# The last item of an attention taken in two parts, with the second part's row maxima beside the first part's exponentials

## The chip, the cores and the metric

The kernel runs on one core of one Trainium2 chip. The metric is device time in microseconds (us) of one execution, as the median over several. TensorE (PE in the profile) multiplies matrices into PSUM, of which there are eight banks of 128 x 512 fp32; VectorE (DVE), ScalarE (ACT) and GpSimd (POOL) work element by element; SyncE (SP) issues the DMA transfers here. Each engine works off its own instructions in order and waits for the others by semaphores.

## The reference

One transformer layer on 2048 rows of 512 columns: 32 heads of 16 columns, and an MLP of 1792 columns with SiLU.

```python
h  = x + softmax_attention(layernorm(x) @ wqkv) @ wo    # 32 heads of 16, scale 1/4
h2 = h + silu(layernorm(h) @ w1) @ w2
```

The softmax is over all 2048 keys, so every query row of every head needs the maximum of 2048 scores before its exponentials.

## The kernel before, in words

Everything is one program of three stages that overlap: layer norm and the projections to q, k and v; the attention; and, for each block of 512 rows (NB = 4), the output projection with wo and the MLP. The attention of the next block runs on around the output of the block before, in one order written out by hand in Python (`for g in range(groups)`, L1049 on).

**Items, groups, chunks.** The attention is cut into 32 *items* (ITEMS): four heads by one block of 512 query rows. An item is 16 *groups*, one for each *chunk* c of 128 keys (KC = 16); group g is chunk g % 16 of item g // 16. A group makes, for its four heads k (HEADS gives each head's place a, j in the tiles), a score product (`scores`, L395: 128 keys x 512 queries into a PSUM bank ps_s, 64 rows of the array) and an exponential on ScalarE into a tile pt; and, two groups later (LAG), four value products (`values`, L656) that add pt into the bank pv, one head in each 32 of its partitions. Row DH of each head's 32 is the sum of the exponentials. After chunk 15 `finish_item` (L671) copies pv to pvs.

**Maxima.** Before an item's exponentials its 64 *maxima* have to be there: `maximum` (L222) multiplies 128 queries by 512 keys of one head in natural order into ps_m (48 rows of the array) and VectorE reduces the 512 columns to one (into mx). j says which half of the array's rows a head uses; a score product and a maximum with the other j can run in the array at the same time. When an item's 64 are found, `finish_max` (L235) takes the maximum over the four key blocks, either on GpSimd, or, where it is urgent, on VectorE (L241), and splits it in two fp16 parts; `place_max` (L264) transposes these, copies them into mt and writes them by two DMAs (L276) into rows 48 and 49 of q's tile qs, so that the score product subtracts them. `due_at` (L306) sets when: jointly in a coming chunk 2 (JOINT), or, if there is none in time, WAIT = 2 steps after the last maximum was found.

**Where maxima stand.** A planner, `maxima(g)` (L1029), says how many (up to three, two in chunk 2) are put beside the four scores of group g: it takes the largest rate at which some coming item would be ready in time, counting off what is set beside the outputs (BESIDE). With three, they stand behind scores 0 to 2, or, if the half (j) that comes first has fewer left than the other, behind scores 1 to 3 (`skip`, L1092). Beside an output's MLP (`mlp`, L823) they stand in bursts: per part f of FC = 14, three after the fifth and three after the last of twelve products (BESIDE_C), and four in the second product, one of those in the bank pv; only in parts f < QUIET of that block, which is 14, 14 and 13. The MLP stands ahead of chunk 0 of items 9, 17 and 25 (`marks`: groups 144, 272, 400), its output projection beside the groups just before.

**The end.** The last item (31) has no maxima beside it. Its VectorE splits the attention's rows of the last block into two fp32r parts (`split_early`) in chunks 0 to 3 and the first two weights w1 in chunk 9. Behind its last group, `finish_last` (L905) transposes pvs, divides by the sums, transposes back (ps_q, o_t, ps_o), makes the last rows of hth and htl of it, projects with wo (ps_wo), and runs the last block's MLP with nothing beside it.

PSUM banks: four for ps_s (`st`), three for ps_m and ps_n (`sm`), one for pv.

Of the kernel before, what the change touches and what calls it, by code (L numbers as in the profile page):

```python
# [48 lines left out]
ITEMS = NB * H // 4  # L49

FIRSTS = 8, 16, 24

# [5 lines left out]

BESIDE = (135, 135, 124)
OUTPUT = 9  # L60
# [12 lines left out]

QUIET = FC, FC, FC - 1


@with_exitstack
def attention_mlp_kernel(ctx: ExitStack, tc: tile.TileContext, x, wqkv, wo, w1, w2, out):
# [134 lines left out]
    def fixed_rows(i):  # L213
        for j in range(2):
# [3 lines left out]
                fix_k[:, None, :].to_broadcast([16, 8, 512]))  # L218

    mx, left = {}, {}  # L220

    def maximum(i, kb, qt, a, j, ps=None):  # L222

        if i not in mx:
            mx[i] = small.tile([P, 2, 2, 4, 4], F32, name="mx", bufs=RING + 1)
            left[i] = 64
# [4 lines left out]
        pin(nc.vector.tensor_reduce(mx[i][:, j, a, qt, kb:kb + 1], ps, axis=AX.X, op=ALU.max))  # L231
        left[i] -= 1
        return left[i] == 0

    def finish_max(i, urgent):  # L235

        nm = small.tile([P, 16], F32, name="nm")
        m4 = mx.pop(i).rearrange("p j a q k -> p (j a q) k")
# [11 lines left out]
        ns = small.tile([P, 2, 2, 8], F16, name="ns")  # L250
        high, rest = (ns[:, :, r, :] for r in range(2))
# [4 lines left out]
        split[i] = ns  # L256

# [5 lines left out]

    def place_max(i):  # L264

        ns = split.pop(i)
        ps = bank("ps_n", "sm", F16)
        tr(ps[:32, :P], ns.rearrange("p j r a -> p (j r a)"), ident_h)
        mt = small.tile([32, P], F16, name="mt")
        if at["attention"]:  # L270
            dve("tensor_copy", mt, ps[:32, :P])
        else:
            act("copy", mt, ps[:32, :P])
# [3 lines left out]
        placed.add(i)  # L277

# [26 lines left out]

    def due_at(i):  # L306
# [5 lines left out]
        return joint - g if joint < KC * i - 2 and joint // KC - 1 not in (-1, *FIRSTS) else WAIT  # L312

    def one_max(half=None, ps=None):

        i = next_item()
        if i == ITEMS:
            return
        if half is None:
            half = at["half"]  # L320
            at["half"] = 1 - half
        if at["blocks"]:

            i = min(range(2), key=lambda n: (todo[n, half] or todo[n, 1 - half] or [(n, KC)])[0][1])
# [5 lines left out]
        found_all = maximum(*todo[i, half].pop(0), ps)  # L330

        finish_rest()
        if found_all:
            steps = due_at(i)
            g = at["group"]
            if g is None or g + 1 in marks:
                soon(steps, place_max, i)
                finish_max(i, g is not None)
                return
            late.setdefault(at["step"] + steps, []).append(i)  # L340
            if steps == WAIT:
                unfinished.append(i)
                found_at["step"] = at["step"]
            else:
                finish_max(i, False)

# [21 lines left out]
    def scores(g, k, kind="st"):  # L368

        i, c = divmod(g, KC)  # L370
        a, j = HEADS[k]
        assert i in placed
# [283 lines left out]
    def values(g):  # L656
        i, c = divmod(g, KC)
        for k in range(4):
            a, j = HEADS[k]
            mm(pv[32 * k:32 * k + DH + 1, :], va[:, c, 4 * (i % 8) + 2 * a + j, :], pts.pop((g, k)),  # L660
               start=c == 0, stop=c == KC - 1)
        if c == KC - 1:
            finish_item(i)

    def place(i, k):
# [5 lines left out]
    def finish_item(i):  # L671

        b, u = divmod(i, 8)
        pvs = bp.tile([P, 512], F32, name="pvs", bufs=1)
        if i == ITEMS - 1:
# [6 lines left out]
        if i == ITEMS - 1:  # L682
            last.append(pvs)
            return
# [10 lines left out]

    rcs, last = {}, []

    def sums(i):
# [206 lines left out]
    def finish_last(pending):  # L905
        b = NB - 1
        for g in pending:
            values(g)
        pvs = last.pop()

        o_t = pt_tile("o_t").rearrange("p (t n) -> p t n", n=P)
        pool("memset", o_t[:, :, :64], 0.0)
        act("activation", small.tile([P, 1], F32, name="sw"), ident[:, :1], AF.Silu)
# [10 lines left out]
        some(0, 3)  # L924
        ps_q, ps_o = (bank(name).rearrange("p (t n) -> p t n", n=P) for name in ("ps_q", "ps_o"))
        for t in range(4):
            tr(ps_q[:, t, :], pvs[:, t * P:(t + 1) * P], ident)
        rc = small.tile([P, 4, 4], F32, name="rl", bufs=1)
        heads = ps_q.rearrange("p t (k r) -> p t k r", r=32)
        dve("reciprocal", rc, heads[:, :, :, DH])  # L930
        for j in range(2):

            to = o_t[:, :, 64:].rearrange("p t (k d) -> p t k d", d=DH)[:, :, 1 - j::2, :]
            dve("tensor_tensor", to, heads[:, :, j::2, :DH],
                rc[:, :, j::2, None].to_broadcast([P, 4, 2, DH]), ALU.mult)
        some(0, 6)
        for t in range(4):
            tr(ps_o[:, t, :], o_t[:, t, :], ident)
        ps_o = ps_o.rearrange("p t n -> p (t n)")[64:]
        act("copy", hth[64:, DC - 1, :], ps_o)  # L940
        low(htl[64:, DC - 1, :], ps_o, hth[64:, DC - 1, :])
        found, parts = {}, {}
# [86 lines left out]
    def maxima(g):  # L1029

        i, c = divmod(g, KC)
        ready = min(ITEMS, i + RING - (0 if c == KC - 1 else 1)) * 64
        rate = max([(64 * (n + 1) - sum(x for x, m in zip(BESIDE, marks) if g <= m <= KC * n) - at["done"])
                    / max(1, KC * n - AHEAD - g) for n in range(i + 1, ITEMS)] or [0])
        if ready < END:
# [13 lines left out]
    for g in range(groups):  # L1049
# [11 lines left out]
        if i in FIRSTS:  # L1061
# [11 lines left out]
            if c == 13:  # L1073
                split_weights("w1", 0, "pool")
        if i == ITEMS - 1:
            if c < 4:
                load_rows(NB - 1, c)
                split_early(c)
            if c == 4:
                for f in range(3):  # L1080
                    load_weights("w1", f)
                load_weights("w2", 0)
                for f in range(2):
                    soon(5, split_weights, "w1", f, "dve", "dve")
        if g == 1:
# [3 lines left out]

        half = 1 - HEADS[g % 2][1]  # L1090
        j = next_item()
        skip = int(n == 3 and j < ITEMS and len(todo[j, half]) < len(todo[j, 1 - half]))  # L1092
        for m in range(4):
            k = m ^ (g % 2)
            if (g, k) not in pts:
                scores(g, k)
            if skip <= m < skip + n:
                one_max(1 - HEADS[k][1])
        if found_at["step"] < at["step"]:
# [45 lines left out]
```

## Time and profile before

| what | us |
|---|---|
| median of 3 runs (1670.39 to 1671.31) | 1670.42 |
| the profiled execution | 1670.46 |
| its span, first to last instruction | 1668.4 |
| PE busy in the span | 1655.0 |
| VectorE busy | 1448.6 |
| ScalarE busy | 1236.4 |
| preparation, up to the first group's scores | 180.5 |
| third output with its MLP, 1215.0 to 1347.7 | 132.7 |
| items 25 to 30, 1347.7 to 1538.4 | 190.7 |
| item 31, 1538.4 to 1571.0 | 32.6 |
| last output and MLP, 1571.0 to 1668.4 | 97.4 |

Times in the views count from the span's start. In a row of the time-ordered view stand the start, the time until the last of the merged instructions ends, the engine, the line, the operation, out<-in, and how many; L85 is the helper that issues every matrix product, L88 every transpose, L102 VectorE's and L99 ScalarE's operations, so that rows are told apart by their tiles. The durations of PE's instructions overlap, since they are pipelined; the distance between starts is what one takes. A row of the windows has the stretch, its length, the busy time of PE, PE's weight loads, VectorE, ScalarE and GpSimd with the number of instructions, the granted clock, and the DMA engines' share and GB/s.

### The profile page before, as it was taken

The numbers are of one execution on the slowest core, as the hardware profiler recorded it, in microseconds if no ns is written. First come the engines' busy times: TensorE is split into PE (matmuls) and PEld (weight loads), VectorE is DVE, ScalarE is ACT, GpSimd is POOL, SyncE is SP. The second block draws the span as 40 slices with busy tenths as digits, with TensorE's granted clock in tenths as the row PEclk, the third lists the DMA queues.
The fourth block names the chain that finished last, engine by engine and source line by source line (L and its number), as shares of the span: only waits on it lengthen the run. The fifth ranks groups of instructions, "written<-read, shape, count | busy, mean of one in ns | idle before, by whom it ended". The sixth has DMA issues, their size and how long they took to land.

```text
span 1668.4 us, 28544 instructions
## 1 busy us (share of the span) xinstructions
PE 1655.0 (99%) x10542; PEld 648.1 (39%) x10542; DVE 1448.6 (87%) x2391; ACT 1236.4 (74%) x2435; POOL 399.0 (24%) x593
## 2 busy tenths in 40 slices
PE   9999999999999999999999999999999999999999
PEld 7666422222245532222245532222245532222387
DVE  7899999999988889999988889999978889997343
ACT  5323799999952389999952279999963279999743
POOL 5423311211234301211244301211234311211200
PEclk9999999999999999999999999999999999999999
DMA  5434411211232211111232111121232111100222
GB/s 199 107 99 140 120 32 37 58 32 37 66 78 67 58 50 35 42 49 33 62 79 74 58 50 32 38 56 32 61 75 80 58 50 32 35 12 21 65 77 81
DMA packets 104403, 102.83 MB, mean 62 GB/s; under 512 B 22732, under 2 KB 81164, under 8 KB 104264
## 3 DMA queue, kind: packets, MB, share of 16 engines
q1 hardware_dynamic: 104264, 101.02, 22.3%
q8 instruction: 82, 1.34, 0.3%
q14 instruction: 57, 0.47, 0.1%
HBM read 77.72 MB, written 17.29 MB: 57 GB/s over the span
## 4 chain that ended last, share of the span: by engine, by line
PE 89%; ACT 5%; DVE 4%; issue 1%; DMA 1%; POOL 0%; SPq 0%; DVEq 0%; POOLq 0%
PE pv L85 34%; PE ps_s L85 20%; PE ps_m L85 11%; PE ps_acc L85 10%; PE ps_qk L85 5%; ACT pt L99 5%; PE ps_wo L85 3%; PE ps_w L85 3%; PE ps_v L85 3%; DVE mx L231 2%; PE ps_tr L88 1%; DVE pvs L102 0%; PE ps_n L88 0%; DVE st L102 0%; SPq L105 0%
## 5 line engine op out<-in xcount | busy, mean ns | idle before, releaser
L231 DVE TENSOR_REDUCE mx<-ps_m 128x1 f32<-128x512 f32 x2009 | 1258.8, 684 | 83.3 <-PE ps_m L85 55.7
L99 ACT ACTIVATE pt<-ps_s 128x512 f32<-128x512 f32 x2048 | 1011.6, 609 | 31.6 <-PE ps_m L85 18.7
L85 PE MATMUL pv<-pt,va 128*17 128x512 f32 x4096 | 537.5, 598 | 1.7 <-DVE pv L102 0.5
L85 PE MATMUL ps_s<-qs,ks 64*128 64x512 f16 x2048 | 531.1, 379 | 3.0 <-ACT pt L99 1.6
L85 PE MATMUL ps_m<-ks,qs 48*128 48x512 f16 x2009 | 501.7, 380 | 0.8 <-DVE mx L231 0.7
L85 PEld LDWEIGHTS <-ks 64*128 64x128 f16 x2048 | 148.6, 95 | 546.9 <-issue 437.6
L92 POOL TENSOR_TENSOR ri<-rc,minus 128x16 f32<-128x16 f32 x31 | 90.6, 2923 | 344.6 <-DMA rc<-dn 344.6
L85 PEld LDWEIGHTS pv<-pt,va 128*17 128x17 f32 x4096 | 68.8, 95 | 217.9 <-issue 204.4
L85 PEld LDWEIGHTS <-qs 48*128 48x128 f16 x2048 | 117.5, 94 | 66.6 <-issue 62.2
L99 ACT CAST w2h<-w 128x512 fp32r<-128x512 f32 x56 | 34.7, 620 | 102.3 <-PE ps_acc L85 102.3
L99 ACT ACTIVATE g<-pv 128x512 f32<-128x512 f32 x39 | 23.3, 597 | 101.9 <-PE pv L85 101.9
L85 PE MATMUL ps_acc<-w2l,gh 128*128 128x512 f32 x224 | 92.9, 415 | 0.0
L85 PE MATMUL ps_acc<-w2h,gh 128*128 128x512 f32 x224 | 92.4, 413 | 0.0
L92 POOL TENSOR_TENSOR w2l<-w,w2h 128x512 fp32r<-128x512 f32 x42 | 53.8, 1282 | 152.7 <-ACT w2h L99 152.7
L85 PE MATMUL ps_acc<-w2h,gl 128*128 128x512 f32 x224 | 88.1, 393 | 0.0
L102 DVE TENSOR_TENSOR gl<-g,gh 128x512 fp32r<-128x512 f32 x53 | 37.1, 700 | 46.7 <-ACT gh L99 46.7
L99 ACT ACTIVATE ks<-ps_qk,qk_s 128x512 f32<-128x512 f32 x30 | 20.7, 690 | 68.8 <-PE ps_qk L85 66.8
L85 PE MATMUL pv<-htl,w1h 128*128 128x512 f32 x156 | 65.6, 420 | 0.0
L85 PE MATMUL pv<-hth,w1h 128*128 128x512 f32 x156 | 62.5, 401 | 0.0
L85 PE MATMUL pv<-hth,w1l 128*128 128x512 f32 x156 | 61.4, 393 | 0.0
L92 POOL TENSOR_SCALAR nm<-nm 128x16 f32<-128x16 f32 x51 | 13.0, 254 | 191.5 <-DVE nm L241 188.2
L92 POOL TENSOR_TENSOR mx<-mx 128x32 f32<-128x32 f32 x38 | 9.5, 250 | 199.1 <-DVE mx L231 197.5
(135 smaller groups left out, 1439.2 us busy)
## 6 DMA issues: line engine op xcount, KB each, us to landing
w<-in_B_w_dram SPq DMA_DIRECT2D x112, 256.0 KB
ks<-kd SPq DMA_DIRECT2D x120, 192.0 KB
qs<-qd SPq DMA_DIRECT2D x128, 48.0 KB
kd<-sh SPq DMA_DIRECT2D x16, 256.0 KB
qd<-sh SPq DMA_DIRECT2D x16, 256.0 KB
hx<-in_A_x_dram SPq DMA_DIRECT2D x16, 256.0 KB
ot<-pvs SPq DMA_DIRECT2D x124, 32.0 KB
den<-dr SPq DMA_DIRECT2D x124, 32.0 KB
```

The source lines that it names most:

```text
L85: tc.keep_in_program_order(nc.tensor.matmul(*a, **k))
L88: tc.keep_in_program_order(nc.tensor.transpose(*a))
L92: tc.keep_in_program_order(getattr(nc.gpsimd, op)(*a, **k))
L99: pin(getattr(nc.scalar, fn)(*a, **k))
L102: pin(getattr(nc.vector, fn)(*a, **k))
L231: pin(nc.vector.tensor_reduce(mx[i][:, j, a, qt, kb:kb + 1], ps, axis=AX.X, op=ALU.max))
```

## The change

Three things, all of them in the order of work; what is computed stays.

1. Item 31 (LAST) is taken in two parts of eight groups: heads with a = 0, then heads with a = 1. A group of it has two heads and two chunks of keys instead of four heads and one chunk (`head`), so that pv holds each head twice, for even and odd chunks. Each part has its own 32 maxima (a *piece*), its own hand-over (nm and ns of 8 and 16 columns, a DMA that writes only that part's half of qs), and its own due time. The first part's pv is copied (`finish_part`), transposed, added, divided and turned back inside the second part (`divide_part`, `turn_part`); `finish_last` does the same for the second part, where it had one division for four heads.
2. The planner's goals: item 31's first 32 maxima are due at its chunk 0, the others at its chunk 8. BESIDE for the third output is 103 in place of 124, and its QUIET 11 in place of 13.
3. With two maxima in a group, and more left in the half that is first, both go to that half, behind scores 0 and 2. The shift with three stays as it was.

In item 31 `split_early` moves from chunks 0 to 3 to chunks 5 to 8, and the two splits of w1 from chunk 9 to chunks 12 and 13.

```diff
-BESIDE = (135, 135, 124)
+BESIDE = (135, 135, 103)
-QUIET = FC, FC, FC - 1
+QUIET = FC, FC, FC - 3
...
+    def head(g, k):
+        i, c = divmod(g, KC)
+        if i < LAST:
+            return *HEADS[k], c
+        return c // HALF, k % 2, c % HALF * 2 + k // 2
+
+    def piece_of(i, a):
+        return i, a if i == LAST else None
...
         for j in range(2):
-            dst = qs[i % RING][64 * j + 48:64 * j + 50].rearrange("r a n -> r (a n)")
-            pin(nc.sync.dma_start(dst.rearrange("r (a b) -> r a b", b=P), mt[16 * j:16 * j + 16, :]))
+            dst = qs[i % RING][64 * j + 48:64 * j + 50, slice(None) if a is None else slice(a, a + 1)]
+            dst = dst.rearrange("r a n -> r (a n)").rearrange("r (a b) -> r a b", b=P)
+            pin(nc.sync.dma_start(dst, mt[n // 2 * j:n // 2 * (j + 1), :]))
...
+    def finish_part():
+        pvs = bp.tile([P, 512], F32, name="pvs", bufs=1)
+        dve("tensor_copy", pvs, pv)
+        o_t = gp.tile([P, 4, P], F32, name="o_t", tag="oh")
+        pool("memset", o_t, 0.0)
+        last.append(o_t)
+        soon(2, divide_part, 0, pvs, o_t, "sm")
+        soon(4, turn_part, 0, o_t, "sm", "dve")
+
+    def divide_part(part, pvs, o_t, kind="st"):
+        ps = bank("ps_q", kind).rearrange("p (t n) -> p t n", n=P)
+        for t in range(4):
+            tr(ps[:, t, :], pvs[:, t * P:(t + 1) * P], ident)
+        halves = ps.rearrange("p t (m j r) -> p t m j r", m=2, r=32)[:, :, :, :, :DH + 1]
+        both = gp.tile([P, 4, P], F32, name="both", tag="ol")[:, :, :2 * (DH + 1)].rearrange("p t (j r) -> p t j r", j=2)
+        rc = small.tile([P, 4, 2], F32, name="rl", bufs=1)
+        dve("tensor_copy", both, halves[:, :, 0])
+        dve("tensor_tensor", both, halves[:, :, 1], both, ALU.add)
+        dve("reciprocal", rc, both[:, :, :, DH])
+        to = o_t[:, :, 64 + 32 * part:96 + 32 * part].rearrange("p t (j d) -> p t j d", j=2)
+        dve("tensor_tensor", to, both[:, :, :, :DH], rc[:, :, :, None].to_broadcast([P, 4, 2, DH]), ALU.mult)
+
+    def turn_part(part, o_t, kind="st", engine="act"):
+        ps = bank("ps_o", kind)
+        for t in range(4):
+            tr(ps[:, t * P:(t + 1) * P], o_t[:, t, :], ident)
+        rows = slice(64 + 32 * part, 96 + 32 * part)
+        if engine == "act":
+            act("copy", hth[rows, DC - 1, :], ps[rows])
+        else:
+            dve("tensor_copy", hth[rows, DC - 1, :], ps[rows])
+        low(htl[rows, DC - 1, :], ps[rows], hth[rows, DC - 1, :])
...
-        ps_q, ps_o = (bank(name).rearrange("p (t n) -> p t n", n=P) for name in ("ps_q", "ps_o"))
...
+        divide_part(1, pvs, o_t)
         some(0, 6)
...
+        turn_part(1, o_t)
...
+        goals = [(64 * (n + 1), KC * n) for n in range(i + 1, LAST)]
+        goals += [(END - 32 * (1 - a), KC * LAST + HALF * a) for a in range(2) if KC * LAST + HALF * a > g]
...
-        skip = int(n == 3 and j < ITEMS and len(todo[j, half]) < len(todo[j, 1 - half]))
+        more = len(todo[j, half]) - len(todo[j, 1 - half]) if j < ITEMS else 0
+        beside = range(n)
+        if n == 3 and more < 0:
+            beside = range(1, 4)
+        if n == 2 and more > 0:
+            beside = 0, 2
```

More of the change, by code (lines that the diff above doesn't have):

```diff
@@ L49 @@
 ITEMS = NB * H // 4
+LAST = ITEMS - 1
+HALF = KC // 2
 FIRSTS = 8, 16, 24
@@ L218, in fixed_rows, with start_of @@
                 fix_k[:, None, :].to_broadcast([16, 8, 512]))
+    def head(g, k):
[5 more added lines that the diff above has]
+        return i, a if i == LAST else None
+    def start_of(piece):
+        i, a = piece
+        return KC * i + HALF * (a or 0)
     mx, left = {}, {}
     def maximum(i, kb, qt, a, j, ps=None):
-        if i not in mx:
-            mx[i] = small.tile([P, 2, 2, 4, 4], F32, name="mx", bufs=RING + 1)
-            left[i] = 64
+        piece = piece_of(i, a)
+        n = 1 if i == LAST else 2
+        if piece not in mx:
+            mx[piece] = small.tile([P, 64], F32, name="mx", bufs=RING + 1)[:, :32 * n].rearrange(
+                "p (j a q k) -> p j a q k", j=2, a=n, k=4)
+            left[piece] = 32 * n
         if ps is None:
@@ L230, in maximum, with finish_max @@
            ks[i % RING][64 * j:64 * j + 48, a, kb * 512:kb * 512 + 512], start=True, stop=True)
[L231 to L238, printed above, removed]
+        pin(nc.vector.tensor_reduce(mx[piece][:, j, a % n, qt, kb:kb + 1], ps, axis=AX.X, op=ALU.max))
+        left[piece] -= 1
+        return left[piece] == 0
+    def finish_max(piece, urgent):
+        m4 = mx.pop(piece).rearrange("p j a q k -> p (j a q) k")
+        rows = m4.shape[1]
+        nm = small.tile([P, 16], F32, name="nm")[:, :rows]
         sign = 1.0
@@ L249, in finish_max @@
                 pool("tensor_tensor", to, to, a, ALU.add)
-        ns = small.tile([P, 2, 2, 8], F16, name="ns")
-        high, rest = (ns[:, :, r, :] for r in range(2))
+        ns = small.tile([P, 32], F16, name="ns")[:, :2 * rows]
+        high, rest = (ns.rearrange("p (j r a) -> p j r a", j=2, r=2)[:, :, r, :] for r in range(2))
         nm = nm.rearrange("p (j a) -> p j a", j=2)
@@ L255, in finish_max @@
         pool("tensor_tensor", rest, nm, high, ALU.subtract)
-        split[i] = ns
+        split[piece] = ns
     placed, split, unfinished, found_at = set(), {}, [], {"step": 0}
@@ L304, in next_item, with due_at @@
         return at["item"]
-    def due_at(i):
+    def due_at(piece):
         g = at["group"]
@@ L311, in due_at @@
         joint = g + WAIT + (JOINT - g - WAIT) % KC
-        return joint - g if joint < KC * i - 2 and joint // KC - 1 not in (-1, *FIRSTS) else WAIT
+        return joint - g if joint < start_of(piece) - 2 and joint // KC - 1 not in (-1, *FIRSTS) else WAIT
     def one_max(half=None, ps=None):
@@ L329, in one_max @@
         at["done"] += 1
-        found_all = maximum(*todo[i, half].pop(0), ps)
+        block = todo[i, half].pop(0)
+        piece = piece_of(i, block[3])
+        found_all = maximum(*block, ps)
         finish_rest()
         if found_all:
-            steps = due_at(i)
+            steps = due_at(piece)
             g = at["group"]
             if g is None or g + 1 in marks:
-                soon(steps, place_max, i)
-                finish_max(i, g is not None)
+                soon(steps, place_max, piece)
+                finish_max(piece, g is not None)
                 return
-            late.setdefault(at["step"] + steps, []).append(i)
+            late.setdefault(at["step"] + steps, []).append(piece)
             if steps == WAIT:
-                unfinished.append(i)
+                unfinished.append(piece)
                 found_at["step"] = at["step"]
             else:
-                finish_max(i, False)
+                finish_max(piece, False)
     def burst(n, *more):
@@ L368, in scores @@
     def scores(g, k, kind="st"):
-        i, c = divmod(g, KC)
-        a, j = HEADS[k]
-        assert i in placed
+        i = g // KC
+        a, j, c = head(g, k)
+        assert piece_of(i, a) in placed
         ps = bank("ps_s", kind)
@@ L908, in finish_last @@
             values(g)
-        pvs = last.pop()
-        o_t = pt_tile("o_t").rearrange("p (t n) -> p t n", n=P)
-        pool("memset", o_t[:, :, :64], 0.0)
+        o_t, pvs = last
         act("activation", small.tile([P, 1], F32, name="sw"), ident[:, :1], AF.Silu)
@@ L924, in finish_last @@
         some(0, 3)
-        ps_q, ps_o = (bank(name).rearrange("p (t n) -> p t n", n=P) for name in ("ps_q", "ps_o"))
[L926 to L935, printed above, removed]
-        some(0, 6)
[L937 to L941, printed above, removed]
+        divide_part(1, pvs, o_t)
+        some(0, 6)
+        turn_part(1, o_t)
         found, parts = {}, {}
@@ L1096, in attention_mlp_kernel @@
                 scores(g, k)
-            if skip <= m < skip + n:
-                one_max(1 - HEADS[k][1])
+            if m in beside:
+                one_max(1 - head(g, k)[1])
         if found_at["step"] < at["step"]:
```

42 lines of the change are left out of this document (24 added, 18 removed).

## The prediction

> **What bounds the kernel now.** I read the page first, then the time-ordered view of TensorE (PE) in one part of an MLP and in the attention, the last item of the attention over all engines, the windows by stage, and the chain of waits behind the last item.
>
> ```profile
> span 1668.4 us, 28544 instructions
> PE 1655.0 (99%) x10542; PEld 648.1 (39%) x10542; DVE 1448.6 (87%) x2391; ACT 1236.4 (74%) x2435; POOL 399.0 (24%) x593
> ```
>
> PE is never idle for long, so what counts is how much PE time each piece takes and what it sits beside. A maximum (a score product into ps_m, then a VectorE reduce into mx) has two very different prices, depending on where it stands.
>
> Beside an output's MLP, where every other product uses the whole array, a burst of maxima is inserted time:
>
> ```profile
> 1329.74 0.39 PE L85 MATMUL pv<-htl,w1h 128*128 128x512 f32 x1
> 1330.06 0.60 PE L85 MATMUL ps_m<-ks,qs 48*128 48x512 f16 x3
> 1330.93 0.40 PE L85 MATMUL ps_acc<-w2h,gl 128*128 128x512 f32 x1
> ...
> 1332.34 0.40 PE L85 MATMUL ps_acc<-w2h,gl 128*128 128x512 f32 x1
> 1332.67 0.60 PE L85 MATMUL ps_m<-ks,qs 48*128 48x512 f16 x3
> 1333.54 0.40 PE L85 MATMUL ps_acc<-w2h,gh 128*128 128x512 f32 x1
> ...
> 1342.01 0.40 PE L85 MATMUL pv<-hth,w1h 128*128 128x512 f32 x1
> 1344.81 0.40 PE L85 MATMUL ps_acc<-w2h,gh 128*128 128x512 f32 x1
> ```
>
> The last two rows stand twelve products apart with nothing between: (1344.81 - 1342.01)/12 = 0.233 us each. From 1329.74 to 1330.93 there are two such steps and a burst of three: 1.19 - 0.47 = 0.72 us. From 1332.34 to 1333.54 two steps and a burst of four (the fourth goes into the bank pv): 1.20 - 0.47 = 0.73 us. So a burst costs 0.73 us, whether of three or four.
>
> In the attention a maximum is free on PE: it runs in the half of the array's rows that the score product beside it leaves empty. There the clock is the group of four scores, three maxima and four value products:
>
> ```profile
> 1417.67 0.39 PE L85 MATMUL ps_s<-qs,ks 64*128 64x512 f16 x2
> 1419.63 0.39 PE L85 MATMUL ps_s<-qs,ks 64*128 64x512 f16 x1
> 1419.86 0.59 PE L85 MATMUL ps_s<-qs,ks 64*128 64x512 f16 x2
> 1420.25 0.37 PE L85 MATMUL ps_m<-ks,qs 48*128 48x512 f16 x1
> 1421.76 0.39 PE L85 MATMUL ps_s<-qs,ks 64*128 64x512 f16 x1
> ...
> 224.22 0.39 PE L85 MATMUL ps_s<-qs,ks 64*128 64x512 f16 x1
> 226.35 0.39 PE L85 MATMUL ps_s<-qs,ks 64*128 64x512 f16 x1
> ...
> 1388.21 0.39 PE L85 MATMUL ps_s<-qs,ks 64*128 64x512 f16 x1
> 1390.17 0.39 PE L85 MATMUL ps_s<-qs,ks 64*128 64x512 f16 x1
> ```
>
> A group takes 1.96 us (1388.21 to 1390.17, chunk 4 of item 26; 1417.67 to 1419.63, chunk 3 of item 27). But chunk 4 of item 27 takes 2.13 us (1419.63 to 1421.76): its third maximum starts at 1420.25, 0.62 after the group's first score, where two slots of 0.23 (1419.63 to 1419.86) would put it at 0.46. That group follows one in which the maxima were shifted by one place (two scores first, in the row 1417.67), so six maxima come with one pause too few, VectorE falls behind, and the third waits for one of the three ps_m banks. The same 2.13 us stands in chunk 4 of item 1 (224.22 to 226.35) and of twelve items in all: 1, 3, 5, 7, 11, 13, 15, 19, 21, 23, 27, 29.
>
> In the last item there are no maxima, and PE could be quick, but ScalarE's exponentials hold it:
>
> ```profile
> 1538.40:1571.00 32.60, 31.47 (x208) 5.70 (x204) 6.08 (x11) 31.60 (x65) 5.88 (x6) 1.00 0.26 74
> ...
> 1539.41 30.59 ACT L99 ACTIVATE pt<-ps_s 128x512 f32<-128x512 f32 x62
> ...
> 1556.63 1.05 PE L85 MATMUL pv<-pt,va 128*17 128x512 f32 x8
> 1557.62 1.04 PE L85 MATMUL ps_s<-qs,ks 64*128 64x512 f16 x4
> ```
>
> 62 exponentials without a gap in 30.59 us are 1.96 us for four. In the window of the item VectorE works 6.08 of 32.60 us, so reduces have room there. PE and ScalarE go round in a closed loop: the scores of a group are spread (1.04 us for four) because the last waits for a bank that an exponential of the group before frees, then come 0.99 us of value products (1556.63 to 1557.62), then the next scores. Work put on PE between value products and scores lengthens that loop.
>
> **The change, part by part.**
>
> *Maxima out of the third output's MLP.* QUIET for it falls from 13 to 11 of 14 parts, and the built programs' orders agree: twenty maxima fewer there (127 to 107 between groups 400 and 402), six bursts in all. 6 x 0.73 = -4.4 us. If only their bare slots counted (two of 0.23 us each), it would be 12 x 0.23 = -2.8. Without bursts a part runs 24 x 0.233 = 5.6 us; the stretch from 1342.01 to 1344.81, which has none, shows no other wait. I take -4.4.
>
> *Those maxima elsewhere.* Fifteen more stand in item 30 and five in the first two groups of item 31, beside scores. On PE and ScalarE they fill what is empty; only the end of item 30 was a little quicker without them:
>
> ```profile
> 1528.31 0.95 PE L85 MATMUL ps_s<-qs,ks 64*128 64x512 f16 x4
> 1536.06 1.04 PE L85 MATMUL ps_s<-qs,ks 64*128 64x512 f16 x4
> ```
>
> Four groups in 7.75 us against 4 x 1.96 = 7.84: +0.1.
>
> *The balance.* With two maxima in an item's chunk 2 and one half behind, both now go to that half (places 0 and 2), and chunk 3 needs no shift. In the built order the shift is gone from all twelve items; their chunks 2 to 4 then hold what the even items hold, which take 1.96 in chunk 4. Chunk 2 has one more slot on PE, four as in any full group, whose value products begin 1.96 - 0.99 = 0.97 after its first score. It is covered:
>
> ```profile
> 1478.66 0.39 PE L85 MATMUL ps_s<-qs,ks 64*128 64x512 f16 x1
> ...
> 1478.97 0.68 DVE L102 COPY pvs<-pv 128x512 f32<-128x512 f32 x1
> ...
> 1479.70 1.05 PE L85 MATMUL pv<-pt,va 128*17 128x512 f32 x8
> ```
>
> In chunk 2 of item 29, which begins at 1478.66, the value products wait until 1479.70 (1.04 after) for VectorE's copy of pv. 12 x 0.17 = -2.0; bound above: 0, if the wait only moves.
>
> *Rushed hand-overs.* When an item's maxima finish too late for a later chunk 2, VectorE makes the last reduce and the copy into mt between running maxima. Before, of the last four items only item 30's was rushed under running maxima (chunk 7 of item 29; item 31's fell where none ran):
>
> ```profile
> 1484.78 0.39 PE L85 MATMUL ps_s<-qs,ks 64*128 64x512 f16 x1
> 1491.01 0.39 PE L85 MATMUL ps_s<-qs,ks 64*128 64x512 f16 x1
> ...
> 1188.22 0.39 PE L85 MATMUL ps_s<-qs,ks 64*128 64x512 f16 x1
> 1190.43 0.39 PE L85 MATMUL ps_s<-qs,ks 64*128 64x512 f16 x1
> ```
>
> Chunks 5 to 7 took 6.23 us, 0.35 more than 3 x 1.96; a hand-over in chunk 13 (item 23) took 2.21, or 0.25 more. Now, twenty maxima later, three are rushed: chunk 8 of item 28, chunk 13 of item 29 and chunk 8 of item 30 (first part of item 31). The second part's falls in chunk 3 of item 31, where VectorE is free. 0.35 + 0.25 + 0.35 - 0.35 = +0.6; bounds -0.35 (none costs) and +0.7.
>
> *The first part's division inside item 31.* One copy of pv (chunk 9), four transposes into ps_q (chunk 11), small VectorE work, four transposes into ps_o (chunk 13), a copy and a subtraction. VectorE has the room shown above, and the splits of w1 and of the attention rows that are put later find it too. The transposes do cost PE time:
>
> ```profile
> 1572.06 0.49 PE ps_q L88 x4
> 1572.55 1.38 PE ps_wo L85 x6
> 1573.93 0.43 PE ps_o L88 x4
> ...
> 1572.59 0.26 DVE L102 RECIPROCAL rl<-ps_q 128x16 f32<-128x16 f32 x1 [0.53 <-PE ps_q L88]
> 1572.88 0.49 DVE L102 TENSOR_TENSOR o_t<-ps_q,rl 128x128 f32<-128x128 f32 x2
> ```
>
> 0.43 to 0.49 us for four, at exactly the place in the loop (after the value products, before the scores) where nothing takes it up. I take 0.5 each: +1.0. Bounds 0 (ScalarE makes it up) and +1.2 (each block also pays the change of array mode that the bursts show: 0.73 less two slots of 0.23 is 0.27 for two changes, 0.13 for one; 2 x (0.46 + 0.13)).
>
> Here a rule is to be weighed. The Trainium skill, TensorEngine Tiling (Array Packing), Tiling Modes, says that a change of tiling mode (not just of tile) drains TensorE. The burst's price beyond its slots agrees; by this rule each transpose block between column-tiled value products and row-tiled scores adds a drain, the edit costs 1.2 instead of 1.0, and the sum below would be 1666.0.
>
> *The tail.* After the last value products the chain of waits above is PE alone: transposes, 1.38 us of ps_wo, transposes. VectorE's reciprocal and two products (1572.59 to 1573.37) hide behind the second ps_wo piece. Now there are four operations (a copy, an addition, the reciprocal, one product), by those rows some 0.26 each, 1.04 against 0.78, ending near 1573.65, before the transposes at 1573.93. So nothing; without that cover +0.3. The shorter copies into hth and htl use fewer partitions and the same columns: no change.
>
> Sum against the profiled execution's 1670.46 (the span of 1668.4 and 2.0 around it; the median of the runs, 1670.42, is the same): -4.4 + 0.1 - 2.0 + 0.6 + 1.0 = -4.7, so **1665.8 us**.
>
> **The rivals.**
>
> *The transposes are absorbed.* ScalarE's four exponentials might run at less than 1.96 without the loop, and it makes up both blocks in the last groups. For it: the end of item 30 ran at 1.94 a group. Against: 0.02 a group over five groups is 0.1. Price: -1.0, so 1664.8.
>
> *The gains stay, but half of them.* The balance only moves its wait to chunk 2 or 3 (0 in place of -2.0), the transposes pay the drain (1.2), the tail loses its cover (0.3): -4.4 + 0.1 + 0.7 + 1.2 + 0.3 = -2.1, so 1668.3, which is no change within 0.2% (3.3 us, about what a measurement of this kernel can tell). Against: the even items show the new arrangement without a wait.
>
> *The second part's maxima arrive late*, the case on the other side. They are written into qs by two DMAs issued in chunk 3 of item 31, and PE waits for them at chunk 8.
>
> ```profile
> 1542.79 0.54 SPq L105 DMA_DIRECT2D dn<-pvs  x1
> 1546.67 0.38 SPq L105 DMA_DIRECT2D rc<-dn  x1
> 1547.56 2.08 SPq L105 DMA_DIRECT2D w<-in_B_w_dram  x4
> ```
>
> The queue is busy there: the pair comes between rc and the four weight loads, at about 1547 to 1548.5, and chunk 8 starts 1538.4 + 8 x 1.96 = 1554.1. rc could be issued when dn had landed, so that a small write takes at most 1546.67 - 1542.79 = 3.9 us: landing by 1552.4, in time. If instead it shared the engines with the 1 MB of weights at the window's 74 GB/s (14 us), it would land near 1562.5, and chunk 8 would wait 8.4 us, with everything behind it: 1665.8 + 8.4 = 1674.2. It turns the sign from a landing at 1554.1 + 4.7 = 1558.8 on.
>
> *The change doesn't do what it says*: excluded as far as order goes, since the built programs show the maxima where the text puts them.
>
> **How the numbers follow.** Forecast 0.6; absorbed 0.17; half the gain 0.18; late 0.05. The first two are faster, though a few costs at their upper bounds could bring the forecast to the edge at 1667.1: faster 0.77, same 0.18, slower 0.05. The bounds at their best give 1670.5 - 4.4 - 2.0 - 0.35 = 1663.7, and at their worst 1670.5 - 2.8 + 0.1 + 0.7 + 1.2 + 0.3 = 1670.0; not all fall together, so the range is 1664.1 to 1668.5.
>
> **What would show it.** In the last two quiet parts of the third MLP, one part in 5.6 us in place of 7.8. Chunk 4 of the twelve items at 1.96, chunk 2 no longer than before. Chunk 8 of items 28 and 30 and chunk 13 of item 29 longer by 0.25 to 0.35. Item 31 about 1 us longer, the step at its chunks 11 and 13. No wait of PE on a DMA at chunk 8. In the tail the second block of transposes with no wait on o_t. The prediction is wrong if chunk 2 of the odd items stretches, or if item 31 grows by much more than the transposes.

## The result and the profile after

The median is **1665.20 us** (1664.61 to 1665.30) against 1670.42 before, a ratio of 0.9967 (95% interval 0.9955 to 0.9979): 5.2 us less, where 4.7 were forecast. The profiled execution, 1664.61, is the quickest of its seven, 0.6 under their median.

The page of the changed kernel, its span and its engines:

```profile
span 1662.8 us, 28572 instructions
PE 1649.5 (99%) x10551; PEld 649.5 (39%) x10551; DVE 1453.2 (87%) x2403; ACT 1235.6 (74%) x2435; POOL 396.7 (24%) x584
```

PE is as full as before and has 5.5 us less to do; what is gone is inserted PE time, not idle time. The places, each in the view in which the prediction looked for it:

**The third MLP.** ScalarE in order of time, first before, then after. SiLU (g) is made once for each MLP part, so that its starts are the clock of the parts. Before:

```profile
1322.41 0.60 ACT L99 ACTIVATE g<-pv 128x512 f32<-128x512 f32 x1 [3.00 <-PE pv L85]
...
1345.01 0.60 ACT L99 ACTIVATE g<-pv 128x512 f32<-128x512 f32 x1 [2.37 <-PE pv L85]
```

After (line numbers have moved: L103 is ScalarE's helper, L106 VectorE's, L89 the products', L92 the transposes'):

```profile
1320.21 0.60 ACT L103 ACTIVATE g<-pv 128x512 f32<-128x512 f32 x1 [2.99 <-PE pv L89]
...
1327.25 0.60 ACT L103 ACTIVATE g<-pv 128x512 f32<-128x512 f32 x1 [1.84 <-PE pv L89]
...
1332.81 0.60 ACT L103 ACTIVATE g<-pv 128x512 f32<-128x512 f32 x1 [1.80 <-PE pv L89]
...
1338.39 0.60 ACT L103 ACTIVATE g<-pv 128x512 f32<-128x512 f32 x1 [2.37 <-PE pv L89]
```

From the first to the last of these starts it took 22.60 us before (1322.41 to 1345.01) and takes 18.18 now (1320.21 to 1338.39): 4.4 less over three parts, two of which have lost their bursts. Parts without bursts run in 5.56 and 5.58, as 24 x 0.233 said.

**The balance.** PE in item 27, chunks 1 to 4 and the start of 5, in the changed kernel:

```profile
1407.07 0.39 PE L89 MATMUL ps_s<-qs,ks 64*128 64x512 f16 x1
1409.14 0.39 PE L89 MATMUL ps_s<-qs,ks 64*128 64x512 f16 x1
1411.13 0.39 PE L89 MATMUL ps_s<-qs,ks 64*128 64x512 f16 x1
1413.09 0.39 PE L89 MATMUL ps_s<-qs,ks 64*128 64x512 f16 x1
1415.05 0.39 PE L89 MATMUL ps_s<-qs,ks 64*128 64x512 f16 x1
```

(Each row is a group's first score.) Chunk 4 takes 1.96 (1413.09 to 1415.05) where it took 2.13; so it does in all twelve items. But four of them, 5, 13, 21 and here 27, keep a little in chunks 1 and 2: 2.07 and 1.99 against 1.96 and 2.02, 0.08 in all (more on this below).

**The rushed hand-overs.** PE in item 28, from the first score of chunk 7 to that of chunk 9:

```profile
1450.39 0.39 PE L89 MATMUL ps_s<-qs,ks 64*128 64x512 f16 x1
1452.46 0.39 PE L89 MATMUL ps_s<-qs,ks 64*128 64x512 f16 x1
1453.67 0.22 PE L92 MATMUL ps_n<-ident_h,ns 128*32 128x128 f16 x1 [0.16 <-DVE mx L253]
1454.67 0.39 PE L89 MATMUL ps_s<-qs,ks 64*128 64x512 f16 x1
```

2.07 and 2.21: 0.36 over two groups of 1.96. PE waits 0.16 us for a bank that VectorE's reduce has not freed, then the transpose ps_n goes ahead.

**Item 31.** PE around the transposes of chunks 11 and 13:

```profile
1551.24 1.04 PE L89 MATMUL ps_s<-qs,ks 64*128 64x512 f16 x4
1552.22 1.05 PE L89 MATMUL pv<-pt,va 128*17 128x512 f32 x8
1553.20 0.66 PE L92 MATMUL ps_q<-ident,pvs 128*128 128x128 f32 x4
1553.79 0.61 PE L89 MATMUL ps_s<-qs,ks 64*128 64x512 f16 x4
...
1556.63 1.05 PE L89 MATMUL pv<-pt,va 128*17 128x512 f32 x8
1557.62 0.66 PE L92 MATMUL ps_o<-ident,o_t 128*128 128x128 f32 x4
1558.21 0.61 PE L89 MATMUL ps_s<-qs,ks 64*128 64x512 f16 x4
```

From value products to scores PE needs 1.57 (1552.22 to 1553.79) and 1.58 us, where it needed 0.99: 0.58 for each block. The scores behind a block no longer spread (0.61 us for four, not 1.04): ScalarE has worked off the scores it had, so the banks that they want are free.

**The tail.** PE ahead of the second block of transposes before, then VectorE and PE there in the changed kernel:

```profile
1573.54 0.39 PE L85 MATMUL ps_wo<-wo_l,hth 128*128 128x512 f32 x1
1573.77 0.60 PE L88 MATMUL ps_o<-ident,o_t 128*128 128x128 f32 x4
```

```profile
1567.21 0.30 DVE L106 COPY both<-ps_q 128x136 f32<-128x136 f32 x1 [0.53 <-PE ps_q L92]
...
1568.11 0.29 DVE L106 TENSOR_TENSOR o_t<-both,rl 128x128 f32<-128x128 f32 x1
1568.18 0.40 PE L89 MATMUL ps_wo<-wo_l,hth 128*128 128x512 f32 x1
1568.46 0.66 PE L92 MATMUL ps_o<-ident,o_t 128*128 128x128 f32 x4
```

The four operations take 1.19 us (1567.21 to 1568.40), and the transposes start 0.28 after the last product (1568.18 to 1568.46) instead of 0.23: the cover is just used up.

### The profile page after: what moved, and what is told of

Same layout as the page of the kernel before. It is cut to its first block, busy times and chain, and to the rows that moved or that the text cites. A ratio compares the mean times of both kernels' runs of the same rounds, so it can differ in the third digit from the quotient of the medians.

```text
span 1662.8 us, 28572 instructions
## 1 busy us (share of the span) xinstructions
PE 1649.5 (99%) x10551; PEld 649.5 (39%) x10551; DVE 1453.2 (87%) x2403; ACT 1235.6 (74%) x2435; POOL 396.7 (24%) x584
## 4 chain that ended last, share of the span: by engine, by line
PE 91%; DVE 4%; ACT 3%; issue 1%; DMA 1%; POOL 1%; SPq 0%; DVEq 0%; POOLq 0%
PE pv L89 35%; PE ps_s L89 21%; PE ps_m L89 11%; PE ps_acc L89 10%; PE ps_qk L89 5%; PE ps_wo L89 3%; PE ps_w L89 3%; ACT pt L103 3%; PE ps_v L89 3%; DVE mx L253 2%; PE ps_tr L92 1%; SPq L109 0%; DVE pvs L106 0%; POOL ri L96 0%; PE ps_n L92 0%
## 5 line engine op out<-in xcount | busy, mean ns | idle before, releaser
L103 ACT ACTIVATE pt<-ps_s 128x512 f32<-128x512 f32 x2048 | 1010.9, 609 | 32.0 <-PE ps_m L89 18.6
L89 PE MATMUL pv<-pt,va 128*17 128x512 f32 x4096 | 537.6, 598 | 1.4 <-DVE pv L106 0.5
L89 PE MATMUL ps_s<-qs,ks 64*128 64x512 f16 x2048 | 532.1, 379 | 2.8 <-ACT pt L103 1.6
L89 PE MATMUL ps_m<-ks,qs 48*128 48x512 f16 x2011 | 504.8, 380 | 0.9 <-DVE mx L253 0.7
L89 PEld LDWEIGHTS <-ks 64*128 64x128 f16 x2048 | 150.2, 95 | 547.2 <-issue 434.2
L89 PEld LDWEIGHTS pv<-pt,va 128*17 128x17 f32 x4096 | 69.0, 95 | 215.3 <-issue 201.6
L89 PEld LDWEIGHTS <-qs 48*128 48x128 f16 x2048 | 119.0, 94 | 63.4 <-issue 57.3
L103 ACT CAST w2h<-w 128x512 fp32r<-128x512 f32 x56 | 34.7, 619 | 99.5 <-PE ps_acc L89 99.5
L103 ACT ACTIVATE g<-pv 128x512 f32<-128x512 f32 x39 | 23.3, 597 | 100.5 <-PE pv L89 100.5
L89 PE MATMUL ps_acc<-w2l,gh 128*128 128x512 f32 x224 | 92.8, 414 | 0.0
L89 PE MATMUL ps_acc<-w2h,gh 128*128 128x512 f32 x224 | 91.9, 410 | 0.0
L89 PE MATMUL ps_acc<-w2h,gl 128*128 128x512 f32 x224 | 88.2, 394 | 0.0
L106 DVE TENSOR_TENSOR gl<-g,gh 128x512 fp32r<-128x512 f32 x53 | 37.2, 701 | 56.2 <-ACT gh L103 56.2
L103 ACT ACTIVATE ks<-ps_qk,qk_s 128x512 f32<-128x512 f32 x30 | 20.7, 689 | 68.8 <-PE ps_qk L89 66.9
L96 POOL TENSOR_SCALAR nm<-nm 128x16 f32<-128x16 f32 (+1 forms) x50 | 12.7, 254 | 232.2 <-DVE nm L264 229.2
L89 PE MATMUL pv<-htl,w1h 128*128 128x512 f32 x156 | 65.5, 420 | 0.0
L89 PE MATMUL pv<-hth,w1h 128*128 128x512 f32 x156 | 62.4, 400 | 0.0
L89 PE MATMUL pv<-hth,w1l 128*128 128x512 f32 x156 | 61.4, 393 | 0.0
L96 POOL TENSOR_TENSOR w1l<-w,w1h 128x512 fp32r<-128x512 f32 x42 | 54.2, 1291 | 11.1 <-ACT w1h L103 11.1
```

The costliest lines, as they stand in the source:

```text
L89: tc.keep_in_program_order(nc.tensor.matmul(*a, **k))
L96: tc.keep_in_program_order(getattr(nc.gpsimd, op)(*a, **k))
L103: pin(getattr(nc.scalar, fn)(*a, **k))
L106: pin(getattr(nc.vector, fn)(*a, **k))
```

## The experiments

Ten kernels, made from the kernel before or the changed one ("after") by a small edit; e8, e9 and e10 put two or three edits together. Beside them the kernel before ran again, "after" did not.

| label | median | range |
|---|---|---|
| before, beside e1 to e4; e5 to e8; e9 and e10 | 1671.12; 1670.47; 1670.50 | |
| after | 1665.20 | 1664.61 to 1665.30 |
| e1_balance_alone | 1668.71 | 1668.57 to 1669.27 |
| e2_without_balance | 1666.33 | 1666.03 to 1667.00 |
| e3_first_part_undivided | 1663.88 | 1663.66 to 1665.62 |
| e4_behind_second_score | 1664.13 | 1663.78 to 1664.73 |
| e5_ten_back | 1666.47 | 1666.09 to 1666.77 |
| e6_relief | 1664.76 | 1664.30 to 1665.07 |
| e7_late_write | 1664.78 | 1664.59 to 1665.67 |
| e8_both | 1664.66 | 1664.02 to 1665.08 |
| e9_relief_weights_later | 1664.35 | 1664.22 to 1664.66 |
| e10_best | 1663.58 | 1663.40 to 1663.95 |

The preparation ahead of the first exponential takes from 179.8 to 180.5 us in the twelve profiled executions, whatever the edit (180.5 before, 179.8 after). So medians that differ by some tenths don't tell two kernels apart; the items and groups in the traces do, which agree to 0.03 us, outside the outputs with their MLP, where nothing was changed.

### The balance, alone and left out

The kernel before with the new `beside` alone:

```diff
-        skip = int(n == 3 and j < ITEMS and len(todo[j, half]) < len(todo[j, 1 - half]))
+        more = len(todo[j, half]) - len(todo[j, 1 - half]) if j < ITEMS else 0
+        beside = range(n)
+        if n == 3 and more < 0:
+            beside = range(1, 4)
+        if n == 2 and more > 0:
+            beside = 0, 2
...
-            if skip <= m < skip + n:
+            if m in beside:
```

> The kernel before with nothing but the new placing of two maxima (scores 0 and 2). Theory: the shift in chunk 3 was what made VectorE late, so chunk 4 of the twelve items goes from 2.13 to 1.96 us and chunk 2 stays at 2.02: 12 x 0.17 = 2.0 us less, 1668.4, or 1668.7 if some of the four items with a step of 0.08 left in chunk 2 (as the changed kernel shows) keep it. Rival: the wait only moves to chunk 2 or 3, 1670.4.

1668.71, a ratio of 0.9986 (0.9977 to 0.9996) to the 1671.12 beside it: 2.4 less by the medians. By the spans of the profiled executions, whose preparations take the same time, it is 1.7 (1668.4 to 1666.7), and the twelve items give as much. PE in its item 27, the first scores of chunks 2 to 5:

```profile
1414.21 0.39 PE L85 MATMUL ps_s<-qs,ks 64*128 64x512 f16 x1
1416.23 0.39 PE L85 MATMUL ps_s<-qs,ks 64*128 64x512 f16 x1
1418.19 0.39 PE L85 MATMUL ps_s<-qs,ks 64*128 64x512 f16 x1
1420.16 0.39 PE L85 MATMUL ps_s<-qs,ks 64*128 64x512 f16 x1
```

2.02, 1.96, 1.97: the wait is gone from chunk 4, and in this item chunk 2 has not grown. The rival falls.

The changed kernel without the two lines `if n == 2 and more > 0: beside = 0, 2`:

> The changed kernel without the new placing of two maxima. Theory: the three parts of the change add up, so this loses what the placing alone gains: 1665.2 + 1.7 to 2.0 = 1666.9 to 1667.2, with 2.13 us back in chunk 4 of the odd items. Rival: with other work around it the placing is worth nothing here, 1665.2.

1666.33 by the median, 1.1 more than after; by the spans of the profiled executions, whose preparations agree here too, 1664.4 against 1662.8, 1.6 more, and 2.13 us are back in chunk 4 of the twelve items. The direction and the place are the theory's; the size is just under it by the spans, and further under it by the medians.

### The first part's division

```diff
-        soon(2, divide_part, 0, pvs, o_t, "sm")
-        soon(4, turn_part, 0, o_t, "sm", "dve")
+        soon(4, blank_part)
+
+    def blank_part():
+        dve("tensor_copy", hth[64:96, DC - 1, :], ones[64:96, :1].to_broadcast([32, 512]))
+        dve("tensor_copy", htl[64:96, DC - 1, :], ones[64:96, :1].to_broadcast([32, 512]))
```

> The changed kernel with the first part's transposes, addition, division and turning back left out; its rows of hth and htl are set to one. Theory: the eight transposes lengthen the closed loop of PE and ScalarE in item 31 by 0.6 us at chunk 10 and 0.5 at chunk 12, and little is made up: 0.9 us less, 1664.3, item 31 at 30.8 us. Rival: the growth of item 31 is its maxima, its copy of pv or ScalarE, and the transposes are absorbed: 1665.2 and item 31 still near 31.7.

1663.88, 1.3 less than after by the medians. ScalarE in order of time, first of the changed kernel, then of this one:

```profile
1530.69 23.13 ACT L103 ACTIVATE pt<-ps_s 128x512 f32<-128x512 f32 x47
1554.22 4.03 ACT L103 ACTIVATE pt<-ps_s 128x512 f32<-128x512 f32 x8 [0.39 <-PE ps_s L89]
1558.63 5.99 ACT L103 ACTIVATE pt<-ps_s 128x512 f32<-128x512 f32 x12 [0.39 <-PE ps_s L89]
```

```profile
1530.68 32.93 ACT L103 ACTIVATE pt<-ps_s 128x512 f32<-128x512 f32 x67
```

The same 67 exponentials end at 1564.62 with the division and at 1563.61 without: 1.0 us. With it ScalarE stands idle twice, 0.39 us each, behind the two blocks; without it, never. So the rest of the two parts (copy of pv, hand-over, sixteen groups of two heads) costs item 31 nothing.

Then the same work in another place: behind the second score of chunks 11 and 13, not ahead of the first.

```diff
...
-        soon(2, divide_part, 0, pvs, o_t, "sm")
-        soon(4, turn_part, 0, o_t, "sm", "dve")
+        between[at["step"] + 2] = divide_part, (0, pvs, o_t, "sm")
+        between[at["step"] + 4] = turn_part, (0, o_t, "sm", "dve")
...
             if m in beside:
                 one_max(1 - head(g, k)[1])
+            if m == 1 and at["step"] in between:
+                fn, args = between.pop(at["step"])
+                fn(*args)
```

> The changed kernel with the two blocks of transposes behind the second score of chunks 11 and 13 instead of ahead of the first. Theory: in item 31 PE waits some 0.35 us ahead of a group's last score for a bank that an exponential frees; work put ahead of that wait is hidden for that much, so a block costs 0.2 instead of 0.55: 0.7 us less, 1664.5. Rival: PE work costs its length wherever it stands (1665.2), or the late third and fourth scores starve ScalarE (1665.5).

1664.13, 1.1 less than after. Its PE and, last, its ScalarE:

```profile
1553.41 0.39 PE L89 MATMUL ps_s<-qs,ks 64*128 64x512 f16 x2
1553.73 0.66 PE L92 MATMUL ps_q<-ident,pvs 128*128 128x128 f32 x4
1554.32 0.39 PE L89 MATMUL ps_s<-qs,ks 64*128 64x512 f16 x2
1554.63 1.05 PE L89 MATMUL pv<-pt,va 128*17 128x512 f32 x8
...
1530.90 33.09 ACT L103 ACTIVATE pt<-ps_s 128x512 f32<-128x512 f32 x67
```

From the first score to the value products 1.22 us (1553.41 to 1554.63) where a group without transposes takes 0.98 (1551.24 to 1552.22 above): 0.24 a block, not 0.58, and the exponentials take 33.09 us, 0.8 less than the 33.93 of after. Nothing was taken out; the transposes now stand where PE had to wait for a bank anyway.

### Maxima in the MLP

```diff
-BESIDE = (135, 135, 103)
+BESIDE = (135, 135, 113)
-QUIET = FC, FC, FC - 3
+QUIET = FC, FC, FC - 2
```

> The changed kernel with ten of the twenty maxima back in the third MLP (QUIET 12, BESIDE 113): three bursts more. Theory: a burst costs 0.73 us whatever stands around it, so +2.2, less up to 0.5 for hand-overs that fall in groups with two maxima: 1666.9 to 1667.4, one MLP part at 7.8 us again. Rival: a burst costs its two slots alone (0.46) and the rest of the gain is elsewhere: +1.4, 1666.6 at most.

1666.47, 1.3 more than after: under the theory's range and within the rival's. The starts of g in the third MLP:

```profile
1320.72 0.60 ACT L103 ACTIVATE g<-pv 128x512 f32<-128x512 f32 x1 [3.02 <-PE pv L89]
1328.50 0.60 ACT L103 ACTIVATE g<-pv 128x512 f32<-128x512 f32 x1 [2.57 <-PE pv L89]
...
1341.08 0.60 ACT L103 ACTIVATE g<-pv 128x512 f32<-128x512 f32 x1 [2.37 <-PE pv L89]
```

20.36 us for three parts against 18.18: +2.18 for three bursts, 0.73 each. The burst's price holds, and so the rival's reading is wrong though its time is nearer; the difference came back later. Items 27 to 30 are 0.85 us shorter than in the changed kernel, more than the 0.5 that was allowed for: the planner puts two maxima in many groups of items 29 and 30, and the hand-overs cost less there. Item 31 is 0.34 longer, since chunk 8 waits for its maxima (see the hand-overs):

```profile
1549.58 0.77 PE L89 MATMUL ps_s<-qs,ks 64*128 64x512 f16 x4 [0.27 <-DMA qs<-mt]
```

### The hand-overs

Two maxima in place of three in a group where a rushed hand-over is due:

```diff
         most = 2 if c == JOINT and i and i - 1 not in FIRSTS else 3
+        if g > 402 and at["step"] in late:
+            most = 2
```

> The changed kernel with two maxima in place of three in the group of each of the three rushed hand-overs (items 28, 29, 30); the three missing ones stand in item 31 (chunks 1 and 2). Theory: the 0.25 us of a hand-over's own group are VectorE's, saturated by three reduces, so a reduce less takes them away: 0.7 us less, 1664.5, those three groups at 1.96. Rival: the step is PE waiting for the split maxima (GpSimd), and a reduce less changes nothing: 1665.2; or item 30's write, one group later, comes too late for its first scores: above 1665.5.

1664.76, 0.4 less than after by the medians, with ranges that overlap. The hand-overs themselves fell as the theory has it: taken from ScalarE's exponentials, items 28 to 30 lost 0.21, 0.11 and 0.31 us, 0.63 in all (chunk 8 of item 28 takes 1.99 in place of 2.21, and item 30 keeps no step over 1.96 but chunk 2's usual 2.02; the wait at the end of item 29, below, is left out of its figure). But two new waits took as much and more back, so that the span of the profiled execution is 1663.3 against 1662.8, with the same preparation; a gain over after isn't shown. PE at the first scores of item 30 and of chunk 8 of item 31, and the queue of SP (SPq, the issues of DMA transfers), in this run:

```profile
1500.01 0.39 PE L89 MATMUL ps_s<-qs,ks 64*128 64x512 f16 x1 [0.40 <-DMA qs<-mt]
...
1547.88 0.79 PE L89 MATMUL ps_s<-qs,ks 64*128 64x512 f16 x4 [0.79 <-DMA qs<-mt]
...
1541.08 2.08 SPq L109 DMA_DIRECT2D w<-in_B_w_dram  x4
1543.59 1.39 SPq L302 DMA_DIRECT2D qs<-mt  x2
```

One group later, the second part's write of qs stands behind the four weight loads of chunk 4, and PE waits 0.79 us for it (item 31's chunk 7 takes 2.82 in place of 1.96): the prediction's case on the other side in miniature. In the changed kernel the write went out just ahead of them:

```profile
1541.20 1.39 SPq L302 DMA_DIRECT2D qs<-mt  x2
1542.69 2.27 SPq L109 DMA_DIRECT2D w<-in_B_w_dram  x4
```

How late may it be? Chunk 6 in place of chunk 3:

```diff
             steps = due_at(piece)
...
+            if piece == (LAST, 1):
+                steps += 3
             late.setdefault(at["step"] + steps, []).append(piece)
-            if steps == WAIT:
+            if steps == WAIT or piece == (LAST, 1):
```

> The changed kernel with the second part's maxima placed in chunk 6 in place of chunk 3 of item 31, behind the weight loads of chunk 4 in the queue. Theory: a small write lands at most 3.9 us after its issue, so the first scores of chunk 8 wait 0 to 2.2 us: 1665.2 to 1667.4, and at chunk 3 there was room of two groups or more. Rival (the prediction's case on the other side): it shares the engines with 1 MB of weights and lands 8 us or more late: 1673 or above.

1664.78, within the range of after. The queue and PE of this run:

```profile
1541.35 2.08 SPq L109 DMA_DIRECT2D w<-in_B_w_dram  x4
1545.03 1.39 SPq L302 DMA_DIRECT2D qs<-mt  x2
...
1547.51 1.01 PE L89 MATMUL ps_s<-qs,ks 64*128 64x512 f16 x4
```

No wait: the pair, issued from 1545.03 to 1546.42, had landed by 1547.51, earlier than the pair of e6, which was issued 1.4 us before it and had landed only at 1547.88. The DMA records of the traces, which hold the start and size of each packet, show why. The pair's packets (sixteen of 256 bytes, the only ones of that size around there) start from 1546.34 to 1547.29 in e6 and from 1546.58 to 1547.12 in e7, in both cases while the last packets of the weights do (until 1547.58 and 1547.22). So what decides is when the weights are through, not when the write is issued behind them. In e7 they are through 0.4 us earlier, and chunk 8 is due 0.5 us later (1547.51, against 1547.88 less the wait, 1547.02). The direct test is the same kernel as e6 with the weights moved behind:

```diff
-            if c == 4:
+            if c == 8:
                 for f in range(3):
                     load_weights("w1", f)
                 load_weights("w2", 0)
                 for f in range(2):
-                    soon(8 + f, split_weights, "w1", f, "dve", "dve")
+                    soon(4 + f, split_weights, "w1", f, "dve", "dve")
```

> The run with relieved hand-overs again, with the four weight loads of item 31 issued in chunk 8 in place of chunk 4 (the splits of w1 stay in chunks 12 and 13). Theory: the 0.86 us at the end of chunk 7 there was the second part's write behind 1 MB of weights in the queue, so with the weights after it the wait is gone and chunk 7 is 1.96: 1664.8 - 0.9 = 1663.9; the 0.46 at the end of item 29 stays, since no weights are there. Rival: the write is late only because its hand-over is one group later (chunk 4): 1664.8 and the wait stays.

1664.35, 0.4 less than e6 by the medians; in the profiled executions item 31's chunk 7 goes from 2.82 to 1.96 us:

```profile
1541.13 1.39 SPq L302 DMA_DIRECT2D qs<-mt  x2
...
1546.96 2.29 SPq L109 DMA_DIRECT2D w<-in_B_w_dram  x4
...
1545.12 1.04 PE L89 MATMUL ps_s<-qs,ks 64*128 64x512 f16 x4
1547.08 1.04 PE L89 MATMUL ps_s<-qs,ks 64*128 64x512 f16 x4
```

The scores of chunk 8 follow those of chunk 7 by 1.96 with no wait, while item 30's write still costs its 0.46. It settles the cause. The source mt is copied at the same place in both runs (until 1540.63 in e6, 1540.69 here); with the weights behind, the pair is issued 2.5 us earlier (1541.13 in place of 1543.59) and its last packet starts 3.9 us earlier (1543.44 in place of 1547.29). Both the wait for SP, which issues the four loads first, and the rest, behind their packets, come of the weights. By the spans of the profiled executions the gain is 0.8 us of the expected 0.9; by the medians it is half of that.

### Together

Transposes as in e4 and two maxima as in e6:

> Transposes behind the second score and the relieved hand-overs together. Theory: the two gains are in different groups and add: 1665.2 - 1.1 (as measured for the transposes) - 0.7 = 1663.4. Rival: the second gain isn't there, 1664.1; or item 30's write is late, above 1664.5.

1664.66: no gain over e4 alone (1664.13), the rival's second case; both late writes are there again, 0.54 and 0.53 us. With the weights in chunk 8 as in e9, and the relief only for `g > 460`, so that item 30's write keeps its time:

> Transposes behind the second score, weights in chunk 8, and two maxima only in the hand-over groups of item 30 and of item 31's first part (not item 29's, so that item 30's write isn't put off). Theory: 1664.1 as with the transposes alone, less 0.25 for each of the two groups: 1663.6, and no wait of PE on a write. Rival: no gain over the transposes alone, 1664.1, since something else is late.

**1663.58**, a ratio to before of 0.9958 (0.9945 to 0.9972): as expected by the median, and the quickest of all, 1.6 under the changed kernel. No score waits for a write. The traces show less of the relief: against e4, items 29 and 30 are 0.35 us shorter, but item 31 is 0.16 longer, since its chunk 1, which now holds three maxima, takes 2.13 us. So 0.2 of the expected 0.5 is shown.

## Why the prediction was right

The forecast of 1665.8 was 0.6 us above the median, well inside the range. Step by step, with the times of the trace:

- *Bursts out of the MLP*: -4.4 forecast, -4.4 measured, and 0.73 a burst again when three were put back.
- *The balance*: -2.0 forecast; -1.7 measured in the changed kernel. Eight items gained 0.17; items 5, 13, 21 and 27 only 0.08 (alone, in e1, item 27 gains 0.17 too). In these four a rushed reduce in chunk 0 makes chunk 1 take 2.07, and the chunk 2 that makes this up without the new placing (1.91) has four slots now and takes 2.00. The step looked at chunks 2 to 4 of an item whose chunk 1 was regular. In items 5, 13 and 21 chunk 2 does stretch, by 0.09, which the prediction named as a sign that it is wrong; it is too little to move the forecast.
- *Hand-overs*: +0.6 forecast; 0.36 + 0.25 + 0.25 less the 0.36 of before is +0.5.
- *Item 30's end* +0.1, as forecast.
- *Division inside item 31*: +1.0 forecast, 1.0 measured by leaving it out. The value taken for a block, 0.5, was a compromise between the bare transposes and the upper bound; the bound was the true price (0.58 a block on PE), and ScalarE made up 0.04 us in each group behind. The Trainium skill, TensorEngine Tiling (Array Packing), Tiling Modes, has the rule that a change of mode drains the array. The 0.58 agrees with it: 0.46 for the transposes and 0.13 for a further change of mode give 0.59. No run takes the two apart.
- *Tail*: 0 forecast, 0.1 measured, from the last exponential to the end of the transposes. The four operations were put at 0.26 each, 1.04 in all, and took 1.19; the chain ends 0.05 after its cover.

These add up to -4.4, where the median says -5.2 and the two spans 1662.8 - 1668.4 = -5.6. The rest of the spans' difference lies outside the forecast's terms: 0.7 in the preparation ahead of the first exponential (180.5 to 179.8 us), some 0.4 in the last MLP, whose instructions the change doesn't touch, and 0.2 that isn't placed. The preparation varies as much between the other profiled executions; what decides it stays open. The median of the changed kernel belongs to a span of 1663.4, so 5.0 of its 5.2 us are in the span; the rest lies outside, where an execution takes 2.0 us before and 1.8 after.

So the mechanism and the places were right, and most terms to 0.1 us. That the total came within 0.6 us of the median is partly luck: the balance, put 0.3 too high, was more than made up by differences outside the forecast's terms.

Of the rivals, *absorbed* is refuted by e3 and e4 (1.0 us of cost, of which 0.8 went by moving it). *Half of the gains* is refuted for the balance by e1. *Late maxima* did not happen, since the write went out ahead of the weights. The mechanism is real and its price was too high: behind the weights the write made chunk 8 0.3 to 0.9 us late in e5, e6 and e8, not 8.4. The forecast gave the 1 MB 14 us at the window's mean rate; in e6 it took 6.5 us from the first load's issue to its last packet (1541.08 to 1547.58).

## What to carry to other kernels

When two engines hold each other in a loop through a few buffers, the cost of added work depends on where it stands in the order: look for the instruction that waits for a buffer, and put the work just ahead of it (0.24 instead of 0.58 us here, for the same transposes). Price an insertion by the distance between its neighbours, not by its own rows, so that the change of array mode is in it. And when a step is put one place later, look at what its transfer then queues behind: here 1 MB of loads for later use made two writes of 2 KB late that a coming group needed.

## What the runs showed of the hardware that was not expected

Two small writes issued behind four loads of 256 KB on the same queue moved only when the loads were almost through, however late they were issued. In e6 they were issued from 0.4 us behind the loads' last issue on (1543.16 to 1543.59), and their last packet started 2.3 us after their own last issue (1544.98 to 1547.29). In e7 they were issued from 1.6 us behind it on (1543.43 to 1545.03), and their last packet started 0.7 us after their own last issue (1546.42 to 1547.12). In both runs this is within 0.3 us of the loads' last packet (1547.58 and 1547.22); in e5 and e8 it is within 0.2. Where the pair stood ahead of the loads, in after, its last packet started 1.0 us after its last issue (1542.59 to 1543.56).

The Trainium skill, DMA: Bandwidth & Descriptors, Two DMAs through the same engine are not ordered, has it that within one queue of one DMA engine descriptors start in order. The packets of e6 and e7 agree with that, though the records don't say which engine carried which packet.
